# Spreading the reciprocal of the denominator by DMA, and moving den and M side by side, in a gated attention and MLP kernel

## The chip, the cores and the metric

The kernel runs on one core of one Trainium2 chip. The metric is the device time of one execution in microseconds (us); a time quoted for a kernel is the median of its runs. "Fast" is the undisturbed state of the chip; only fast runs are compared.

The engines: PE is TensorE's matrix products, PEld its weight loads, DVE is VectorE, ACT is ScalarE, POOL is GpSimd, and SP is the engine whose queue issues nearly all DMAs here.

## The reference, cut to what matters

```python
def _A_ref(x, wqkv, wo):                      # S = 2048, D = 640, 32 heads of 20
    ...
    pq, pk = phi(q), phi(k)
    kv  = jnp.einsum("bhsd,bhse->bhde", pk, v)
    z   = jnp.einsum("bhsd->bhd", pk)
    num = jnp.einsum("bhqd,bhde->bhqe", pq, kv)
    den = jnp.einsum("bhqd,bhd->bhq", pq, z)[..., None] + 1e-6
    o = num / den
    return (...o as [B, S, D]...) @ wo
def _B_ref(x, w1, w2, w3, w4): ...            # layernorm, W1, shift, W2, layernorm, W3, W4
g = sigmoid((x * gate_w).sum(-1))
out = g * _A_ref(...) + (1 - g) * _B_ref(...)
```

The division by `den` is one number for each head and token. The kernel computes the reciprocal as 32 rows (heads) times 2048 tokens, and needs it on all 128 partitions to scale `pq`: every head's row is wanted on four partitions. That spreading is what the change is about.

## The kernel before

Tokens are handled in four tiles of 512 (t = 0 to 3). PSUM is the memory that TensorE writes its results to. Below, den is the denominator, M is the product of each head's kv with `wo`, and W1 to W4 are the products of the MLP. The parts that the argument touches:

```python
ps = ctx.enter_context(tc.tile_pool(name="ps", bufs=4, space=PSUM))
def pair():                                    # a PSUM pair; four of them rotate
    return ps.tile([P, 2, 512], F32, name="pp")

def w1_unit(t, fcs):                           # 5 products of 512 columns for each fc, then gelu
    pt = pair()
    for i, fc in enumerate(fcs):
        for dc in range(DC):
            ...
            nc.tensor.matmul(pt[:, i, :], lhsT=w, rhs=lnxT[t][:, dc, :], ...)
    ...
def den_mm():                                  # 20 products, 32 columns of the array each
    pt = pair()
    for j in range(DC):
        for t in range(NT):
            nc.tensor.matmul(pt[32 * t:32 * (t + 1), 0, :], lhsT=zbd[:, j, :],
                             rhs=pqT[:, j, t * TS:(t + 1) * TS], ...)
    return pt
def den_evac(pt):
    nc.scalar.activation(pt[:, 1, :], pt[:, 0, :], ACT.Copy, bias=1e-6)
    nc.vector.reciprocal(r_bf[:], pt[:, 1, :])
def r_unit():                                  # 4 products, 32 rows of the array each
    pts = [pair(), pair()]
    for t in range(NT):
        nc.tensor.matmul(pts[t // 2][:, t % 2, :], lhsT=emat[32 * t:32 * (t + 1), :],
                         rhs=r_bf[32 * t:32 * (t + 1), :], start=True, stop=True)
    for k in range(2):
        nc.scalar.copy(rb[:, 2 * k:2 * k + 2, :], pts[k][:])
def m_unit(j):                                 # 16 products, 32 columns of the array each
    pt = pair()
    for hf in range(2):
        for p in range(2):
            for q in range(4):
                nc.tensor.matmul(pt[32 * q:32 * (q + 1), hf, 0:HD], lhsT=kvT[:, 2 * q + p, j, :], ...)
    nc.scalar.copy(m_sb[:, j, :]..., pt[:, :, 0:HD])
# cut: the order of the stretch in question
for fcs in w1_split:                           # W1 of tile 0: ((0, 1), (2, 3), (4,))
    w1_unit(0, fcs)
kv_unit()
den_evac(den_mm())
for cc in range(CPT):
    ln1_apply(3 * CPT + cc)                    # layernorm of tile 3, each ends in a DMA transpose
for fcs in w1_split:
    w1_unit(1, fcs)
...
for j in range(DC):
    m_unit(j)
r_unit()
# then W2 of tile 0, W1 of tiles 2 and 3 (scale_t multiplies pqT by rb on DVE), W3, ...
```

Three forms of TensorE's array are in play: the full array (W1, kv, W2), four tiles of 32 columns (den, M), and four tiles of 32 rows (the spreading products).

## Time and profile before

Time 265.61 us (three runs, 265.43 to 266.17). The page of the profile, its share of busy time, granted clock (in tenths, 40 slices) and the summary of the chain that ended last:

```profile
...
PE 260.3 (99%) x1744; PEld 161.8 (61%) x1744; DVE 139.5 (53%) x271; ACT 85.1 (32%) x126; POOL 21.9 (8%) x67
...
PEclk9999999999999999999999999999999999999999
...
PE 97%; ACT 1%; DVE 0%; issue 0%
...
```

TensorE is busy for 99% of the span at full clock, and 97% of the chain of waits is TensorE's. The list of waits of PE has one line (who waited for whom: us in total, times, longest):

```profile
...
PE pp L206 <- PEq L589: 0.8, 1, 0.8
```

The stretch that the change touches, from the timeline of PE (start in us, us until its last product ends, engine, line, operation, output<-inputs, shape, count). Products overlap, so lengths of stages are differences of starts:

```profile
...
71.28 4.48 PE L345 MATMUL pp<-lnxT,w_sb 128*128 128x512 bf16 x20
...
76.67 1.60 PE L364 MATMUL pp<-wk_sb,m_sb 128*128 128x120 bf16 x30
78.19 1.26 PE L251 MATMUL pp<-pqT,zbd 128*32 128x512 bf16 x20
79.39 4.49 PE L345 MATMUL pp<-lnxT,w_sb 128*128 128x512 bf16 x20
...
84.89 2.90 PE L383 MATMUL pp<-wo_sb,kvT 128*32 128x320 bf16 x80
87.72 0.40 PE L263 MATMUL pp<-r_bf,emat 32*128 32x512 bf16 x4
88.20 5.59 PE L417 MATMUL pp<-w_sb,hsT 128*128 128x320 bf16 x40
...
```

| Stage (before) | us between starts | products |
|---|---|---|
| W1 of tile 0 | 5.39 | 25 of 512 columns, 0.2156 each |
| kv | 1.52 | 30 |
| den | 1.20 | 20, four at a time |
| W1 of tile 1 | 5.50 | 25 |
| M | 2.83 | 80, four at a time |
| spreading products | 0.48 | 4, at once |
| whole stretch, W1 of tile 0 to W2 | 16.92 | |

The same place in the chain of waits (start, us, what):

```profile
...
84.96 0.69 PE pp L383 x16
85.65 0.02 issue
85.67 2.49 ACT m_sb L385 x4
88.16 0.04 issue
88.20 5.59 PE pp L417 x40
...
```

Here ACT stands in the chain: from 85.67 to 88.16 it goes over four of ACT's copies of M, into W2's start at 88.20.

DVE's timeline shows the reciprocal, and W2's first sum:

```profile
...
80.17 3.36 DVE L258 RECIPROCAL r_bf<-pp 128x512 bf16<-128x512 f32 x1
...
89.76 0.82 DVE L420 TENSOR_TENSOR x<-pp,x_sb 128x640 f32<-128x640 f32 x1 [2.94 <-PE pp L417]
...
```

SP's timeline shows the transposes of the first layernorm for tiles 2 and 3 (line 303), and those of the second layernorm of tile 0 (line 436):

```profile
...
74.63 16.46 SPq L303 DMA_TRANSPOSE lnxT<-ln  x8
94.58 6.89 SPq L436 DMA_TRANSPOSE lnxT<-ln  x4
...
```

### The profile page before, as it was taken

To read this page: it belongs to the slowest core of one execution; us is meant where nothing else is said; L and a number is where in the kernel's file an instruction comes from. 1 tells how busy PE (TensorE), PEld (TensorE's weight loads), DVE (VectorE), ACT (ScalarE), POOL (GpSimd) and SP (SyncE) were. 2 spreads that over 40 slices of the span, in tenths; PEclk is the share of its full clock that TensorE was granted. 3 is DMA by queue.
4 is the path that set the end of the run, shared out by engine and by line. 5 is a ranking of instruction groups with operands and counts; after the bars stand their busy time and mean duration, and the time that the engine had idled before them with its cause. 6 is when DMAs were issued, how large, how long until landed. Compare 5 with 4: busy or idle time off the path is not lost.

```text
span 264.0 us, 4272 instructions
## 1 busy us (share of the span) xinstructions
PE 260.3 (99%) x1744; PEld 161.8 (61%) x1744; DVE 139.5 (53%) x271; ACT 85.1 (32%) x126; POOL 21.9 (8%) x67
## 2 busy tenths in 40 slices
PE   8999999999999999999999999999999999999995
PEld 4777555788754654556667555667565576555743
DVE  1688778899948597964503455413356223112132
ACT  1555554321165725612502221412131332142100
POOL 7100120012210040001000001000001000000000
PEclk9999999999999999999999999999999999999999
DMA  7999987016673726700132000051100051100011
GB/s 200 179 208 370 375 252 298 0 29 123 124 101 75 79 51 161 239 0 2 25 75 77 25 0 2 0 99 52 50 0 2 0 101 52 50 0 2 0 50 50
DMA packets 46285, 23.62 MB, mean 89 GB/s; under 512 B 35770, under 2 KB 45626, under 8 KB 46266
## 3 DMA queue, kind: packets, MB, share of 16 engines
q1 hardware_dynamic: 45824, 22.86, 34.1%
q10 hardware_dynamic: 442, 0.49, 0.5%
q8 instruction: 13, 0.21, 0.4%
q14 instruction: 6, 0.05, 0.1%
HBM read 12.21 MB, written 2.62 MB: 56 GB/s over the span
## 4 chain that ended last, share of the span: by engine, by line
PE 97%; ACT 1%; DVE 0%; issue 0%
PE pp L484 21%; PE pp L464 21%; PE pp L194 8%; PE pp L311 8%; PE pp L417 8%; PE pp L448 8%; PE pp L345 8%; PE pp L236 8%; PE pp L206 2%; PE pp L472 1%; PE pp L493 1%; ACT m_sb L385 1%; PE pp L364 1%; PE pp L251 0%; DVE oc L512 0%; PE pp L383 0%
## 5 line engine op out<-in xcount | busy, mean ns | idle before, releaser
L464 PE MATMUL pp<-lnxT,w_sb 128*128 128x512 bf16 x260 | 60.4, 379 | 0.0
L484 PE MATMUL pp<-w_sb,h 128*128 128x256 bf16 (+3 forms) x416 | 58.0, 299 | 0.1
L466 ACT ACTIVATE h<-pp 128x1024 bf16<-128x1024 f32 (+1 forms) x28 | 26.9, 962 | 82.2 <-PE pp L464 82.2
L484 PEld LDWEIGHTS <-h 128*128 128x128 bf16 x416 | 39.3, 98 | 18.0 <-issue 1.3
L464 PEld LDWEIGHTS <-w_sb 128*128 128x128 bf16 x260 | 25.5, 98 | 26.8
L500 DVE SCALAR_TENSOR_TENSOR oc<-pp,omg,x 128x640 bf16<-128x640 f32 x14 | 12.0, 881 | 41.4 <-ACT h2x L475 21.3
L451 DVE SCALAR_TENSOR_TENSOR x<-pp,gate,x 128x640 f32<-128x640 f32 x16 | 13.9, 868 | 29.4 <-PE pp L448 29.4
L420 DVE TENSOR_TENSOR x<-pp,x_sb 128x640 f32<-128x640 f32 x16 | 13.1, 820 | 22.6 <-PE pp L417 22.6
L186 ACT ACTIVATE e<-pp 128x640 bf16<-128x640 f32 (+1 forms) x26 | 21.5, 827 | 9.6 <-PE pp L236 9.6
L448 PE MATMUL pp<-m_sb,pqT 128*128 128x320 bf16 x160 | 24.3, 299 | 0.0
L417 PE MATMUL pp<-w_sb,hsT 128*128 128x320 bf16 x160 | 23.9, 299 | 0.1
L194 PE MATMUL pp<-wk_sb,xT 128*128 128x320 bf16 (+1 forms) x160 | 22.9, 302 | 0.0
L311 PE MATMUL pp<-x_sb,pk 128*128 128x320 bf16 (+1 forms) x160 | 22.3, 300 | 0.0
L236 PE MATMUL pp<-xT,hsT 128*128 128x512 bf16 x100 | 21.7, 379 | 0.0
L311 PEld LDWEIGHTS <-pk 128*128 128x128 bf16 x160 | 18.8, 117 | 3.5
L417 PEld LDWEIGHTS <-hsT 128*128 128x128 bf16 x160 | 15.6, 98 | 8.2 <-issue 0.2
L448 PEld LDWEIGHTS <-pqT 128*128 128x128 bf16 x160 | 15.7, 98 | 7.7
L194 PEld LDWEIGHTS <-xT 128*128 128x128 bf16 x160 | 15.8, 99 | 6.1
L345 PE MATMUL pp<-lnxT,w_sb 128*128 128x512 bf16 x80 | 17.9, 379 | 0.0
L236 PEld LDWEIGHTS <-hsT 128*128 128x128 bf16 x100 | 11.8, 118 | 9.7
L281 POOL TENSOR_SCALAR rstd<-mv 128x4 f32<-128x4 f32 (+1 forms) x11 | 3.4, 314 | 156.5 <-DVE mv L287 156.5
L188 DVE SCALAR_TENSOR_TENSOR pk<-pp,e 128x640 bf16<-128x640 f32 x16 | 13.2, 825 | 1.7
(77 smaller groups left out, 194.9 us busy)
## 6 DMA issues: line engine op xcount, KB each, us to landing
out_dram<-oc SPq DMA_DIRECT2D x14, 160.0 KB, 1.8
w_sb<-in_B_w_dram SPq DMA_DIRECT2D x1, 2080.0 KB, 10.0
w_sb<-in_B_w_dram SPq DMA_DIRECT2D x1, 1296.0 KB, 8.4
x_sb<-in_A_x_dram SPq DMA_DIRECT2D x2, 640.0 KB, 10.4
x_sb<-in_A_x_dram SPq DMA_DIRECT2D x1, 1120.0 KB, 7.9
wo_sb<-in_A_wo_dram SPq DMA_DIRECT2D x6, 160.0 KB, 6.0
w_sb<-in_B_w_dram SPq DMA_DIRECT2D x1, 864.0 KB, 5.7
hsT<-in_A_wqkv_dram SPq DMA_DIRECT2D x1, 800.0 KB, 5.3
```

Of the source, the lines that this page charges most:

```text
L186: nc.scalar.activation(ev, src, ACT.Exp)
L188: nc.vector.scalar_tensor_tensor(dst, src, 0.0, ev, op0=ALU.max, op1=ALU.add)
L194: nc.tensor.matmul(pt[:, hf, 0:n], lhsT=xT[:, dc, c * P:(c + 1) * P], rhs=wk_sb[:, dc, hf * HD:hf * HD + n], start=(dc == 0), stop=(dc == ...
L236: nc.tensor.matmul(pt[:, t % 2, :], lhsT=wq_sb[:, dc, :].rearrange("p (m j) -> p j m", j=DC)[:, j], rhs=xT[:, dc, t * TS:(t + 1) * TS], st ...
L311: nc.tensor.matmul(pt[:, hf, 0:HD + hf], lhsT=w, rhs=x_sb[:, c, hf * HD:(hf + 1) * HD + hf], start=(c == 0), stop=(c == NCH - 1))
L345: nc.tensor.matmul(pt[:, i, :], lhsT=w, rhs=lnxT[t][:, dc, :], start=(dc == 0), stop=(dc == DC - 1))
L417: nc.tensor.matmul(pt[:, hf, 0:HD], lhsT=hsT[:, fc, 2 + c * P:2 + (c + 1) * P], rhs=w2_sb[:, fc, hf * HD:(hf + 1) * HD], start=(fc == 0), ...
L448: nc.tensor.matmul(pt[:, hf, 0:HD], lhsT=pqT[:, j, c * P:(c + 1) * P], rhs=m_sb[:, j, hf * HD:(hf + 1) * HD], start=(j == 0), stop=(j == D ...
L451: nc.vector.scalar_tensor_tensor(x1, pt[:, :, 0:HD], gate[:, c:c + 1], x1, op0=ALU.mult, op1=ALU.add)
L464: nc.tensor.matmul(pt[:, k, :], lhsT=w3_sb[:, dc, fc * P:(fc + 1) * P], rhs=lnT[:, dc, :], start=(dc == 0), stop=(dc == DC - 1))
L466: nc.scalar.activation(h2[:, 2 * i * TS:(2 * i + n) * TS], pt[:].rearrange("p h e -> p (h e)")[:, 0:n * TS], ACT.Gelu_apprx_tanh)
L484: nc.tensor.matmul(dst, lhsT=st[t]["h2"][:, fc * TS + cc * P:fc * TS + (cc + 1) * P], rhs=w4_sb[:, fc, a:b], start=start and fc == 0, stop ...
```

## The change

The intent is to take the four spreading products off the bottleneck engine: DVE copies the reciprocal's four bands into one tile of 32 partitions, and four DMAs write it to partitions i, i+4, i+8 and so on. Den and M are put side by side behind the first W1 unit of tile 1, so that the array keeps its form. Epsilon is added by DVE instead of ACT. Loads are merged, to make room for the four DMAs on SP.

```diff
 def den_evac(pt):
-    nc.scalar.activation(pt[:, 1, :], pt[:, 0, :], ACT.Copy, bias=1e-6)
+    d = e_p.tile([P, 1024], BF16, name="e")[:].bitcast(F32)
+    nc.vector.tensor_scalar_add(d, pt[:, 0, :], 1e-6)
-    nc.vector.reciprocal(r_bf[:], pt[:, 1, :])
-
-def r_unit():
-    ... (four products, two ACT copies)
+    nc.vector.reciprocal(r_bf[:], d)
+    for t in range(NT):
+        nc.vector.tensor_copy(r4[:, t, :], r_bf[H * t:H * (t + 1), :])
+    for i in range(4):
+        nc.sync.dma_start(rb[bass.ds(i, H, 4), :, :], r4[:])
 ...
 kv_unit()
+w1_unit(1, w1_split[0])
 den_evac(den_mm())
+for j in range(DC):
+    m_unit(j)
 for cc in range(CPT):
     ln1_apply(3 * CPT + cc)
-for fcs in w1_split:
+for fcs in w1_split[1:]:
     w1_unit(1, fcs)
 ...
-for j in range(DC):
-    m_unit(j)
-r_unit()
 ...  (cut: x, wv, w1 and w3 loaded in one DMA each where there were two;
       the masks emat gone; kvT's memset and the copies to w1x split otherwise)
```

More of the change, by code (lines that the diff above doesn't have):

```diff
@@ L85 @@
     r_bf = const.tile([P, TS], BF16)
+    r4 = const.tile([H, NT, TS], BF16)
     ident = const.tile([P, P], BF16)
@@ L90 @@
     zbd = const.tile([P, DC, H], BF16)
-    emat = const.tile([P, P], BF16)
     bmask = const.tile([P, GH * 4], F32)
@@ L136 @@
     load_x(1, 8)
-    load_x(8, 12)
-    load_x(12, 16)
-    for a, b in ((0, 2), (2, DC)):
-        sp.dma_start(wv_sb[:, a:b, :], wqkv_v[:, a:b, 2 * D:3 * D])
-    for a, b in ((0, 2), (2, DC)):
-        sp.dma_start(w1_sb[:, a:b, :], B_w1[a * P:b * P, :].rearrange("(c p) f -> p c f", p=P))
+    load_x(8, 16)
+    sp.dma_start(wv_sb[:], wqkv_v[:, :, 2 * D:3 * D])
+    sp.dma_start(w1_sb[:], B_w1.rearrange("(c p) f -> p c f", p=P))
     for g in range(NG):
@@ L147 @@
         sp.dma_start(w2_sb[32 * g:32 * (g + 1), 4, :], B_w2[CG * g + P:CG * (g + 1), :])
-    for a, b in ((0, 2), (2, DC)):
-        sp.dma_start(w3_sb[:, a:b, :], B_w3[a * P:b * P, :].rearrange("(c p) f -> p c f", p=P))
+    sp.dma_start(w3_sb[:], B_w3.rearrange("(c p) f -> p c f", p=P))
     nc.gpsimd.memset(mhalf[:], -0.5)
@@ L161 @@
                             base=3, pattern=[[4, H]], channel_multiplier=-1)
-    nc.gpsimd.memset(emat[:], 1.0)
-    for t in range(4):
-        sl = emat[32 * t:32 * (t + 1), :]
-        nc.gpsimd.affine_select(out=sl, in_=sl, compare_op=ALU.is_ge, fill=0.0,
-                                base=0, pattern=[[1, P]], channel_multiplier=-4)
-        nc.gpsimd.affine_select(out=sl, in_=sl, compare_op=ALU.is_ge, fill=0.0,
-                                base=3, pattern=[[-1, P]], channel_multiplier=4)
     for m, n, off in ((bmask, GH, 0), (bmask5, 2, 88)):
@@ L174 @@
                                 base=off + Dh - 1, pattern=[[Dh, n], [0, 4]], channel_multiplier=-1)
-    nc.gpsimd.memset(kvT[:], 0.0)
-    for a, b in ((0, 1), (1, 2), (2, 3), (3, DC)):
+    for b in range(0, len(pairs_qg), 2):
+        nc.gpsimd.memset(kvT[:, b:b + 2], 0.0)
+    for dc in range(DC):
         for g in range(4):
-            nc.gpsimd.tensor_copy(w1x[:, a:b, 32 * g:32 * (g + 1)], w1_sb[:, a:b, CG * g + P:CG * (g + 1)])
+            nc.gpsimd.tensor_copy(w1x[:, dc, 32 * g:32 * (g + 1)], w1_sb[:, dc, CG * g + P:CG * (g + 1)])
     def phi(dst, src, n):
@@ L255, in den_evac @@
     def den_evac(pt):
-        nc.scalar.activation(pt[:, 1, :], pt[:, 0, :], ACT.Copy, bias=1e-6)
+        d = e_p.tile([P, 1024], BF16, name="e")[:].bitcast(F32)
+        nc.vector.tensor_scalar_add(d, pt[:, 0, :], 1e-6)
         with nc.allow_low_precision(reason="rounded after a float32 division, as a copy would"):
-            nc.vector.reciprocal(r_bf[:], pt[:, 1, :])
-    def r_unit():
-        pts = [pair(), pair()]
+            nc.vector.reciprocal(r_bf[:], d)
         for t in range(NT):
-            nc.tensor.matmul(pts[t // 2][:, t % 2, :], lhsT=emat[32 * t:32 * (t + 1), :],
-                             rhs=r_bf[32 * t:32 * (t + 1), :], start=True, stop=True)
-        for k in range(2):
-            nc.scalar.copy(rb[:, 2 * k:2 * k + 2, :], pts[k][:])
+            nc.vector.tensor_copy(r4[:, t, :], r_bf[H * t:H * (t + 1), :])
+        for i in range(4):
+            nc.sync.dma_start(rb[bass.ds(i, H, 4), :, :], r4[:])
     def scale_t(t):
```

## The prediction

> **What bounds the kernel now.** TensorE. The page shows PE busy 260.3 of 264.0 us (99%) at a granted clock of 1.00; the chain that ended last is 97% PE; the list of waits shows one PE wait in the whole program, 0.8 us at the start. So only PE work, PE joints or a new PE wait change the time.
>
> **The stretch concerned**, read from the timeline of PE starts: W1 of tile 0 5.39 us, kv 1.52, den 1.20, W1 of tile 1 5.50, M 2.83, spread of the reciprocal (4 products) 0.48, W2 of tile 0 5.43.
>
> The four products each take 0.384 us but overlap: PE is busy 0.40 us with all four. The Trainium skill ("TensorE: Matmul & The Clock Gate", Part 3) says products on different 32-row groups run concurrently; this trace agrees. So they are worth 0.48 us, not 1.5.
>
> Joints: a W1 product is issued every 0.216 us, so 25 take 5.39; tile 1's W1 takes 5.50 after den. Den's five rounds of 4 should take 1.08, took 1.20. M's 20 rounds at 0.1357 should take 2.71, took 2.83. So entering or leaving the 32-column form costs about 0.1 us, and PEld sits idle 0.4 us at such places. Den beside M means one excursion, not two.
>
> **Removed:** the 4 products (0.48 us of PE, critical); three ACT copies (1.07, 1.07, 0.58) and masks on POOL: none critical.
>
> **Added:** DVE add of epsilon (estimate 0.65 us, from 0.82 for 640 float32 columns), four 32x512 copies (1.19 us, as the four hx copies take), four DMAs of 128 KB issued by SP (about 0.5 us each, landing within about 2 us). The reciprocal stays 3.36 us. The merged loads and split POOL copies run well before their readers: no effect.
>
> **New order in time:** the first W1 unit (2.16) covers the kvT masking (78.85 to 80.13), so M can start at once after den, near 81.6. DVE: add to 82.4, reciprocal to 85.8, copies to 87.0, four layernorms to 88.4, hx copies to 89.8, then W2's first sum at 89.8, as before (89.76). PE reaches W2 near 87.6 instead of 88.20. Hence:
> - Den's PSUM pair is freed near 82.4, needed near 83.3.
> - W2's fourth unit needs the hx copies near 92; they end near 89.8.
> - rb lands near 91; the scaling reads it after 101.
> - Tile 3's transposes are issued about 5 us later, near 88.5 to 94. Their reader, W1 of tile 3, starts near 98.4.
> - Tightest: the last transpose of tile 0's second layernorm was issued at 100.3 and lands 2.6 us later, 102.9; W3 started at 104.42, now near 103.9. Slack about 1 us, less if DVE slips.
>
> So I expect no new PE wait, and the saving to be the 0.48 us plus one joint, 0.5 to 0.7.
>
> **Predicted: 265.0 us, 264.3 to 265.7 (8 in 10). Chances: faster by over 2% 0.01, within 2% 0.97, slower by over 2% 0.02.**
>
> **What would show each step.** PE start of W2 near 87.6; PE busy lower by about 0.5 us; W3's first start about 0.5 to 0.6 us earlier; den plus M about 3.9 us together against 4.03 apart; the DVE scaling at about the same time as before (101.35).
>
> **What would make it wrong.** A PE wait for tile 3's or W3's first transposes (SP held by the rb DMAs, or rb DMAs colliding with transposes); W2 waiting for DVE; M waiting for kvT or den's pair. Each would cost about 0.5 to 3 us, under 2%. Run-to-run spread is 0.7 us.

## The result, and the profile after

The time after is 265.28 us (four runs, 265.21 to 265.60); before, with one more run, 265.73 us. Ratios in this document are the mean time of one kernel's fast runs over that of the other's fast runs of the same rounds, so not quite the ratio of the medians quoted. Here it is 0.9984, with a 95% interval of 0.9967 to 1.0001. The change was run again later (below): 265.26 against 265.91 us, ratio 0.9985 (0.9961 to 1.0010). So the change is within 2%, as predicted; the two ratios agree on about 0.4 us, each with an interval that just reaches 1.

The page after, busy time and the summary of the chain:

```profile
...
PE 258.4 (98%) x1722; PEld 161.0 (61%) x1740; DVE 141.4 (54%) x276; ACT 82.7 (31%) x123; POOL 20.2 (8%) x65
...
PE 92%; SPq 3%; DMA 3%; issue 1%; DVE 0%
...
```

PE's busy time fell by 1.9 us, but this number can't be used: 1722 products are on the record, where the change took away 4 of 1744. The others are records that the trace lacks. Starts of stages don't suffer from that. (The chain's 3% for SP and for DMA are from the first loads at the program's start, not from the stretch.)

PE's timeline after:

```profile
...
71.41 4.48 PE L332 MATMUL pp<-lnxT,w_sb 128*128 128x512 bf16 x19
...
76.81 1.60 PE L351 MATMUL pp<-wk_sb,m_sb 128*128 128x120 bf16 x30
78.25 2.32 PE L332 MATMUL pp<-lnxT,w_sb 128*128 128x512 bf16 x9
80.50 1.26 PE L241 MATMUL pp<-pqT,zbd 128*32 128x512 bf16 x20
81.59 2.89 PE L370 MATMUL pp<-wo_sb,kvT 128*32 128x320 bf16 x80
84.41 2.33 PE L332 MATMUL pp<-lnxT,w_sb 128*128 128x512 bf16 x9
...
87.66 5.60 PE L403 MATMUL pp<-w_sb,hsT 128*128 128x320 bf16 x40
...
103.88 2.32 PE L450 MATMUL pp<-lnxT,w_sb 128*128 128x512 bf16 x9
...
```

From W1 of tile 0 to W2 it is now 87.66 - 71.41 = 16.25 us, 0.67 us less than 16.92. Den takes 1.09 and M 2.82, together 3.91, where it was 1.20 and 2.83. W1 of tile 0 itself began 0.13 us later than in the profile of before, so W3 starts only 0.54 us earlier (103.88 against 104.42), and so does the end.

PE's list of waits has three lines more than before:

```profile
...
PE pp L184 <- DMA wk_sb<-in_A_wqkv_dram: 0.2, 1, 0.2
PE pp L470 <- issue: 0.2, 1, 0.2
PE pp L184 <- DMA xT<-in_A_x_dram: 0.2, 1, 0.2
```

The two waits for DMA are for the program's first loads (the first at 5.83 us), long before the stretch. The line with `issue` stands in all nine profiles that lack products and in none of the five that have them all, so it is most likely a gap in the record.

In the chain of waits ACT has gone from this place; between M and W2 there are products only:

```profile
...
81.76 2.72 PE pp L370 x80
...
87.82 5.43 PE pp L403 x40
...
```

DVE has the new addition, the reciprocal, and the copies; W2's first sum comes at the time it came before:

```profile
...
81.81 0.69 DVE L247 TENSOR_SCALAR e<-pp 128x512 f32<-128x512 f32 x1 [1.56 <-PE pp L241]
82.54 3.35 DVE L249 RECIPROCAL r_bf<-e 128x512 bf16<-128x512 f32 x1
85.93 1.17 DVE L251 COPY r<-r_bf 32x512 bf16<-32x512 bf16 x4
...
89.78 0.82 DVE L406 TENSOR_TENSOR x<-pp,x_sb 128x640 f32<-128x640 f32 x1
...
```

The reciprocal takes the same from SBUF as from PSUM (3.35 against 3.36 us). On SP, the four new DMAs (line 253), tile 3's transposes (line 290) and those of the second layernorm (line 422):

```profile
...
87.13 2.50 SPq L253 DMA_DIRECT2D rb<-r  x4
89.73 5.22 SPq L290 DMA_TRANSPOSE lnxT<-ln  x4
95.49 5.99 SPq L422 DMA_TRANSPOSE lnxT<-ln  x4
...
```

Each of the four DMAs holds SP for about 0.59 us and lands 2.6 to 3.4 us after its issue. Tile 3's transposes start at 89.73; the second layernorm's first transpose is issued at 95.49, after 94.58 before, because it now queues behind them. Its reader, W3, started without a wait.

### The profile page after: what moved, and what is told of

It is laid out like the page before. It is cut to its first block, busy times and chain, and to the rows that moved or that the text cites. A ratio compares the mean times of both kernels' runs of the same rounds, so it can differ in the third digit from the quotient of the medians.

```text
span 263.5 us, 4244 instructions
## 1 busy us (share of the span) xinstructions
PE 258.4 (98%) x1722; PEld 161.0 (61%) x1740; DVE 141.4 (54%) x276; ACT 82.7 (31%) x123; POOL 20.2 (8%) x65
## 4 chain that ended last, share of the span: by engine, by line
PE 92%; SPq 3%; DMA 3%; issue 1%; DVE 0%
PE pp L470 21%; PE pp L450 21%; PE pp L298 8%; PE pp L434 8%; PE pp L403 8%; PE pp L332 8%; PE pp L226 8%; PE pp L184 4%; DMA xT<-in_A_x_dram 3%; SPq L121 3%; PE pp L370 1%; PE pp L458 1%; PE pp L479 1%; PE pp L351 1%; PE pp L241 0%
## 5 line engine op out<-in xcount | busy, mean ns | idle before, releaser
L177 DVE TENSOR_SCALAR e<-e 128x640 bf16<-128x640 bf16 (+1 forms) x26 | 9.5, 367 | 8.9 <-ACT e L176 7.5
```

## The experiments

The first question is what the 0.67 us consist of. The theory: columns of the products, plus a fixed price each time the array changes its form. Rivals: all of it is the products, or it comes from the relief of ACT and DVE. The main measure is the stretch from the first W1 product of tile 0 to the first product of W2, because whole times turned out to carry noise from both ends of the program.

### Run 1: the DMA spread alone

```diff
 (kernel before)
     nc.vector.reciprocal(r_bf[:], pt[:, 1, :])
+    (the four copies and the four DMAs)
-r_unit()
```

> Kernel before, with only the four spreading products and their two ACT copies replaced by the four DVE copies and four DMAs; den and M stay apart. Theory (the gain is PE work plus joints of the array's form): the four products and the joint between row form and full form go, the exit joint of M stays: W2 starts 0.45 to 0.5 us earlier relative to the start of W1 of tile 0 than in before (16.4 against 16.92 us), time 0.4 to 0.5 us less. Rival A (all of the gain is the products): the whole 0.67 us. Rival B (the gain comes from ACT or DVE relief): anything else.

The stretch was 88.17 - 71.72 = 16.45 us, 0.47 us shorter than before. So the products with what hangs on them are worth 0.47, not the whole 0.67. The time, however, was 265.83 us against 265.80, ratio 1.0007 (0.9988 to 1.0026): the expected 0.4 to 0.5 us was not seen, and the interval leaves room for 0.3 us at most. In this profile the program's end took 0.7 us longer; runs 10 and 12 return to that.

### Run 2: the order alone

```diff
 (kernel after)
-    (the four copies and the four DMAs)
+def r_unit(): ... (as before)
 for fcs in w1_split[1:]:
     w1_unit(1, fcs)
+r_unit()
```

> Kernel after, but the reciprocal is spread by the four products again, right before W2; den and M stay side by side behind the first W1 unit of tile 1. Theory: two joints less than before, stretch from W1 of tile 0 to W2 16.7 us or a little less (0.2 us less than 16.92), and the four products again 0.4 to 0.5 us. Rival A: 16.92, no gain from order.

The stretch was 88.05 - 71.39 = 16.66 us, 0.26 less than before; time 265.98, ratio 1.0012 (0.9995 to 1.0029). The products cost less here than in before. PE's timeline of this run, the products and W2:

```profile
...
87.73 0.39 PE L261 MATMUL pp<-r_bf,emat 32*128 32x512 bf16 x4
88.05 5.61 PE L415 MATMUL pp<-w_sb,hsT 128*128 128x320 bf16 x40
...
```

That is 0.32 us from their start to W2's, where 0.4 to 0.5 was expected and before had 0.48 for the very same four products.

### Runs 3 and 5: the products four times, and twice

```diff
 (kernel before)
-    for t in range(NT):
+    for t in list(range(NT)) * 4:      # and * 2
         nc.tensor.matmul(pts[t // 2][:, t % 2, :], lhsT=emat[...], rhs=r_bf[...], ...)
```

> Kernel before, with the four spreading products issued four times over (same result). Theory: four concurrent products cost the columns of one, 0.216 us, and the rest of their 0.48 us is the joint, paid once: each of the three extra rounds adds 0.22 us, 0.65 us in all (0.48 becomes 1.13). Rival: the 0.48 us is all cost of the products, then 1.4 us more; if they were not concurrent, 2.6 us more.

> Kernel before, with the four spreading products issued twice. The run with four rounds added 0.50 us to the stretch, not 0.65, and its chain of waits has no ACT piece, where that of before goes over four ACT copies of M (2.49 us) into W2. Theory (in before W2 waits about 0.15 us for ACT to free the PSUM pair of M's fourth unit, and a second round of products hides in that wait): M to W2 0.216 times 2 plus 0.12, 0.55 us against 0.48, only 0.07 more. Rival (each round simply costs 0.167): 0.65 us.

The timelines of PE, first with four rounds:

```profile
...
88.17 1.04 PE L263 MATMUL pp<-r_bf,emat 32*128 32x512 bf16 x16
89.15 5.61 PE L417 MATMUL pp<-w_sb,hsT 128*128 128x320 bf16 x40
...
```

and with two:

```profile
...
87.61 0.61 PE L263 MATMUL pp<-r_bf,emat 32*128 32x512 bf16 x8
88.15 5.61 PE L417 MATMUL pp<-w_sb,hsT 128*128 128x320 bf16 x40
...
```

Four rounds take 0.98 us, two 0.54, one took 0.48. So four rounds added 0.50 us and not the expected 0.65. From two to four it is 0.22 us for each round, one product's 512 columns; from one to two only 0.06. So with one round some 0.15 us of PE's time was no work. The chain of waits names it: in before it goes over ACT's copies of M into W2, with two and four rounds there is no ACT in that place. Four PSUM pairs rotate; W2's first unit takes the pair of M's fourth unit, and before waited for ACT to empty it. A second round of products hides in that wait. The weight loads show the same wait directly. The timeline of weight loads (PEld) in before has W2's first one at 88.05:

```profile
...
88.05 0.93 PEld L417 LDWEIGHTS <-hsT 128*128 128x128 bf16 x7 [0.23 <-issue]
```

W2's first product started at 88.20, 0.15 us after it; in runs 1, 2, 3 and 5, which change form there too, the two starts lie within 0.01 us of each other. It was not less work on ACT that removed the wait: in run 1 ACT's copies of M began 14.39 us after W1 of tile 0, just as in before, and W2 started at 88.17, before the fourth of them had ended (near 88.6).

The rival, 0.167 us for each round, is refuted by the run with two rounds (0.54 measured, 0.65 expected). Time with four rounds 266.64, ratio 1.0033 (1.0017 to 1.0050), which is the 0.5 us of the stretch and some noise.

### Run 4: M put apart again

```diff
 (kernel after)
-for j in range(DC):
-    m_unit(j)
 ...
-for fcs in w1_split[1:]:
-    w1_unit(1, fcs)
+for fc in (2, 3, 4):
+    w1_unit(1, (fc,))
+    m_unit(fc - 2)
+for j in (3, 4):
+    m_unit(j)
```

> Kernel after, but den, the first three M units and the last two are put apart by five or ten W1 products each (three W1 units of one PSUM half), so the array enters and leaves the 32-column form four times instead of once. Theory (0.2 us for one entry and exit): three more excursions, the stretch from W1 of tile 0 to W2 grows from 16.25 to about 16.85 us, time 0.6 us more than after. Rival (joints cost nothing, the saving came from elsewhere): 16.25 and the time of after.

The stretch was 88.32 - 71.42 = 16.90 us, 0.65 more than after, for three more entries and exits. PE's timeline around two of them:

```profile
...
82.89 0.73 PE L370 MATMUL pp<-wo_sb,kvT 128*32 128x320 bf16 x16
83.55 1.25 PE L332 MATMUL pp<-lnxT,w_sb 128*128 128x512 bf16 x5
84.73 0.73 PE L370 MATMUL pp<-wo_sb,kvT 128*32 128x320 bf16 x16
...
```

An M unit of 16 products should take 4 x 0.1357 = 0.54 (0.1357 us is what a W2 product of 320 columns takes, four M products go at once); it takes 0.66. Five W1 products should take 1.08; they take 1.18. The time was 265.68, ratio 1.0002 (0.9976 to 1.0027): against the 265.28 of after, from another job, this is 0.4 us more, in line, but not resolved by so few runs.

With this the stretch can be written as a sum. Its work is 50 W1 products at 0.2156, kv 1.43 (the chain's number), five rounds of den at 0.2156, 20 rounds of M at 0.1357: 16.00 us, plus 0.22 for each round of spreading products. The rest, divided by the changes of form:

| Kernel | stretch, us | work, us | rest, us | changes of form | rest for each |
|---|---|---|---|---|---|
| after | 16.25 | 16.00 | 0.25 | 2 | 0.12 |
| order alone | 16.66 | 16.22 | 0.44 | 4 | 0.11 |
| DMA spread alone | 16.45 | 16.00 | 0.45 | 4 | 0.11 |
| products twice | 16.99 | 16.43 | 0.56 | 5 | 0.11 |
| products four times | 17.43 | 16.86 | 0.57 | 5 | 0.11 |
| M apart | 16.90 | 16.00 | 0.90 | 8 | 0.11 |
| before | 16.92 | 16.22 | 0.70 | 5 | 0.14 |

Six kernels agree on 0.11 to 0.12 us for each change of form. Before is the only one out of line, by 0.70 - 5 x 0.112 = 0.14 us: the wait for ACT. So the 0.67 us are 0.22 of columns, three changes of form (0.33), and the lost wait (0.14); these add up to 0.69. A change of stage that keeps the form costs almost nothing: in after, den to M takes 1.09 us for 1.08 of work, and the last W1 unit to W2 1.08 for 1.08. Before was profiled once, so its 0.48 rests on one profile; its stages up to the products (16.44 us) agree with runs 3 and 5 (16.45 each).

### Run 6: epsilon back in PSUM

```diff
 (kernel after)
-    d = e_p.tile(...); nc.vector.tensor_scalar_add(d, pt[:, 0, :], 1e-6)
-    nc.vector.reciprocal(r_bf[:], d)
+    nc.scalar.activation(pt[:, 1, :], pt[:, 0, :], ACT.Copy, bias=1e-6)
+    nc.vector.reciprocal(r_bf[:], pt[:, 1, :])
```

> Kernel after, but epsilon is added by ACT within PSUM and the reciprocal reads PSUM, as in before. Theory (DVE's add only frees a PSUM pair early; the built program lets M rotate over the three other pairs, and W2's first unit waits for the reciprocal, done near 85.8): no PE wait, W1 of tile 0 to W2 16.25 us as after, 0 to 0.2 us longer if an ACT copy is late. Rival (M's fourth unit must wait for the reciprocal): 2.4 us longer.

The stretch was 87.69 - 71.44 = 16.25 us and the time 265.30 us, ratio 0.9981 (0.9962 to 0.9999), the same as after. Moving epsilon to DVE is worth nothing here, in either direction. The wait that one would fear, M's fourth unit for den's pair, does not come.

### Run 7: the old loads

```diff
 (kernel after)
-    (merged loads of x, wv, w1, w3; split memset and w1x copies)
+    (those of before)
```

> Kernel after, with the loads, the memset and the w1x copies of before. Theory (these parts run long before their readers): stage times and W1's start as in after apart from the start of the program, where four runs put W1 of tile 0 at 71.28 to 71.72 whatever the kernel; time within 0.3 us of after. Rival (merged loads shift the start): W1 of tile 0 starts at 71.28 as in before, the two early waits for DMA of after (0.2 us each) are gone.

The stretch was 16.25 us again. W1 of tile 0 started at 71.69, so the start was not the one of before, and the early waits of after are not tied to merged loads either (one of them was seen in the run with the products twice, which has the old loads). The time was 265.69, ratio 0.9992 (0.9970 to 1.0014), 0.4 us more than after and so just outside the expected 0.3, and again the program's end was 0.7 us longer.

### Runs 8 and 11: the four DMAs three times, and twice

This measures how much slack SP's queue had.

```diff
 (kernel after)
-    for i in range(4):
+    for i in list(range(4)) * 3:       # and * 2
         nc.sync.dma_start(rb[bass.ds(i, H, 4), :, :], r4[:])
```

> Kernel after, with the four DMAs of the reciprocal issued three times (same result), to measure the slack of the SP queue behind them. Each DMA costs SP 0.59 us to issue, and each round waits for the landing of the round before, so tile 3's transposes should be issued 5 to 5.5 us later, near 95 to 100, the last landing near 101.7; W1 of tile 3, which would start at 98.5, then waits about 3 us, and W3 starts about 3 us later. If the queue had more slack than I think: no wait and the time of after.

> Kernel after with the four DMAs issued twice. From the run with three rounds (last transpose of tile 3 landed near 102.7, each extra round about 2.8 to 3.3 us): tile 3's transposes issued near 92.6 to 97.8, the last landing near 99.2, so W1 of tile 3 waits 0.3 to 0.8 us, W3 up to 0.8 us later than in after. A wait this short should leave the granted clock at 1.0, where the wait of 3.8 us took it to 0.994 and made the next twenty products 1.4 us longer.

PE's timeline with three rounds, W1 of tile 3:

```profile
...
102.78 5.92 PE L332 MATMUL pp<-lnxT,w_sb 128*128 128x512 bf16 x20 [3.82 <-DMA lnxT<-ln]
...
```

with two rounds:

```profile
...
100.25 4.48 PE L332 MATMUL pp<-lnxT,w_sb 128*128 128x512 bf16 x20 [1.47 <-DMA lnxT<-ln]
...
```

With two rounds the wait was 1.47 us, more than expected, because SP needed 6.3 us for eight issues with their waits, not 5. The first transpose of tile 3 was issued 3.83 us later than in after (93.56 against 89.73), and W1 of tile 0 had itself started 0.14 us later, so the slack was 3.83 - 0.14 - 1.47 = 2.2 us. With three rounds the same sum gives 6.20 - 0.31 - 3.82 = 2.1 us. So the change has spent most of the slack of tile 3's transposes, and about 2 us are left.

With three rounds W3 started at 109.61, 5.7 us later than in after (about 3 was expected), though the wait was 3.8. The view of windows, for the wait and for the stretch after it (window; busy us and instructions of PE, PEld, DVE, ACT and POOL; granted clock; share of DMA busy; GB/s):

```profile
...
98.96:102.78 3.82, 0.00 (x1) 0.03 (x1) 3.55 (x7) 0.64 (x2) 0.93 (x2) 0.94 0.62 123
102.78:108.53 5.75, 5.75 (x20) 2.30 (x21) 4.86 (x12) 1.09 (x2) 1.16 (x3) 0.74 0.53 104
...
```

The twenty products after the wait took 5.75 us instead of 4.31, at a mean granted clock of 0.74 (0.50 up to 105.5 us, 1.00 from 106.0 on). With two rounds, after a wait of 1.47 us, they took 4.31 at 1.00. The Trainium skill ("TensorE: Matmul & The Clock Gate", Part 1, "What's actually happening") says that the clock falls to half after an idle window of about 3.4 us; both runs, one profile each, are in line with it. The times of these single runs were 270.92 and 267.63 us.

### Runs 9, 10 and 12: the time again, and the program's ends

> Kernel after once more, unchanged, for the time and the spread at both ends. Theory: W1 of tile 0 to W2 16.25 us again; W1 of tile 0 starts anywhere from 71.2 to 71.7 (TensorE's first products run slow for a time that differs from run to run), W3 to the end of the span 159.6 to 160.3; time 0.3 to 0.7 us less than before, ratio 0.997 to 0.999.

> The kernel with the DMA spread alone once more, which saved 0.47 us in its stretch and nothing in the time of its first four runs. Theory (the time of that job lost the gain to the start and the end, which differ from run to run): stretch 16.45 us again, time 0.2 to 0.5 us less than before, between before and after. Rival (the DMA spread costs something outside of the stretch when done alone): time equal to before again, and a stage of the profile outside of start and end is longer.

> The DMA spread alone, but with the merged loads of after, so that SP has as many DMAs as in before (96 in the two runs with the spread alone and the old loads, 92 here and in before). In eleven profiles the time from DVE's last operation to the end of the span was 2.3 us in all seven kernels with 92 SP DMAs, 3.0 us in the three runs with 96 and the old loads. Theory (the DMA spread is worth its 0.47 us, and the program's end, which follows SP's stream and not the work, took it back): stretch 16.45 us, end 2.3 us, time 0.3 to 0.6 us less than before, ratio about 0.998. Rival (the spread alone itself makes the end longer): end 3.0 us again, time equal to before.

Run 9 is the kernel after, unchanged. Run 10 is the kernel of run 1, unchanged. Run 12 has this edit:

```diff
 (kernel of run 1, DMA spread alone)
-    (x, wv, w1 and w3 loaded in two DMAs each: 96 DMAs on SP)
+    (the merged loads of the changed kernel: 92 DMAs on SP, as in before)
```

Run 9 repeated the change: stretch 16.24, time 265.26 (six runs, 265.04 to 267.14) against 265.91.

Runs 10 and 12 repeated the stretch of the DMA spread alone, 87.49 - 71.04 = 16.45 and 87.40 - 70.95 = 16.45, and neither is measurably faster than before: 265.95 against 265.91, ratio 0.9997 (0.9985 to 1.0009), and 265.75 against 266.05, ratio 0.9996 (0.9983 to 1.0009). So neither shows the expected 0.2 to 0.6 us; the intervals leave room for at most 0.40 and 0.45 us. The two ends of the program explain why such a gain is hard to see:

- The start. TensorE's first products run slow, for a time that differs: two products of 320 columns took 0.54 us at 4.82 in before and 0.28 at 6.08, but 0.27 already at 4.72 in run 12. (The granted clock on record reads 1.00 there all the same; the slow phase is read from the products' starts.) In fourteen profiles W1 of tile 0 started anywhere from 70.95 to 71.72 us, and kernels with the same code up to there (before, and the products twice and four times) have 71.28, 71.16 and 71.72. The skill describes such a start (same page and section: the activity window runs freely, so the point of change varies by 500 ns either way). Waits for the first loads can add to it: the profile of after has two of 0.2 us.
- The end. From DVE's last operation to the end of the span it takes 2.3 us in before, after, and five other kernels, but 3.0 or 3.1 in runs 1, 7 and 10, 2.7 in run 12, 2.6 in runs 2 and 11.

SP's list of waits shows the end. Its last two waits (us in total, times, longest), before, then run 10:

```profile
...
SPq L600 <- DMA out_dram<-oc: 0.8, 1, 0.8
...
SPq L600 <- PEq L600: 0.6, 2, 0.4
...
```

```profile
...
SPq L588 <- DMA out_dram<-oc: 1.1, 1, 1.1
SPq L588 <- PEq L588: 1.0, 2, 0.5
...
```

The wait for the last output's DMA grew from 0.8 to 1.1 us, and that for PE's sequencer from 0.6 to 1.0. Both are after all work is done. I had guessed that this follows the number of DMAs on SP, because all seven profiles with 92 had the short end, and the three with 96 and the old loads the long one. Run 12 has 92 and an end of 2.7 us, with the first wait short (0.8) and the second long (1.0). So the guess is at best half right; what sets the end in a given build stays open. It does not touch the change: before and after both have the short end of 2.3 us.

One run of before took 705.72 us; it was slow and is not used.

No version better than the changed kernel came out of this. What is left in the stretch over the bare work is 0.25 us, two changes of form; run 6 equals the changed kernel.

## Why the prediction was right

The predicted time was 265.0 us, 264.3 to 265.7; measured 265.28. The class, within 2%, was right, but says little: any change of less than 5 us would have met it, and the interval of the time reaches 1. The evidence is the stretch. There the mechanism was right for most points:

- **TensorE bounds.** Right. In the profiled runs the span fell by 0.5 us, the stretch's 0.67 less the 0.13 of its later start, and nothing of the relief of ACT and POOL shows elsewhere. Run 6 shows it for the ACT operation with epsilon.
- **Size in the stretch, 0.5 to 0.7 us.** Right, 0.67. The split was less good. "So they are worth 0.48 us" took the whole gap from the products' start to W2's as a cost of the products. It was 0.22 of columns, 0.14 of waiting for ACT to free a PSUM pair, and a change of form. The wait stood in the chain of waits before ("ACT m_sb L385 x4", 2.49 us), and I had not used it: the list of waits has no line for it, since the products' modelled ends cover all but 0.08 us of the gap. "The list of waits shows one PE wait in the whole program" was true of the list and not of the kernel. That the sum came out right was partly luck: the wait and the change of form, not known to be part of the 0.48, went away together with the products (run 1 saved 0.47).
- **Joints of about 0.1 us.** Right: 0.11 to 0.12 for each change of form. Three fewer give 0.33 us, where the prediction counted one excursion at about 0.1 to 0.2 beside the products; the change of form that went with the products was hidden in their 0.48.
- **No new PE wait.** Right; runs 8 and 11 show that about 2 us of slack are left for tile 3's transposes. The prediction called W3's transposes the tightest place with about 1 us; with the DMAs doubled, W1 of tile 3 was the first to wait, for 1.47 us, and W3 waited only 0.2 us after it.
- **Times of the stages.** W2 at 87.66 (predicted 87.6), W3 at 103.88 (103.9), den plus M 3.91 (3.9), W2's first sum on DVE at 89.78 (89.8). Tile 3's transposes came at 89.73 instead of 88.5, behind SP's four DMAs, which were first issued at 87.13 and took 2.5 us, where I had counted 2; even with 2 us, from copies done at 87.0, the prediction's own numbers give 89.0. The DVE scaling came at 101.37 (before 101.35), as predicted.
- **PE busy lower by about 0.5 us.** Not usable: 1.9 us lower, with products missing from the record.
- **The spread between runs.** "Run-to-run spread is 0.7 us" was taken as noise of no origin. Two parts of it were found: the slow first products at the start, and the program's end, which differs between builds.

The time came out 0.3 us above the predicted one. In the profiled run 0.13 us of that is the later start of the stretch; the rest is within the spread, and not explained.

## What to carry to other kernels

On a kernel bound by TensorE, small products on tiles of the array cost their columns once for four, plus about 0.11 us for every change of the array's form around them; put those of one form side by side, and count changes as carefully as products. A gap between two stages on a busy engine is not all work: look in the chain of waits for another engine before you price it, and double the suspected cost, as a wait shows by swallowing the first addition. For gains below the noise of whole times, compare a stretch within the profile that begins and ends at fixed products.

## What the Trainium skill lacked or had wrong

- "TensorEngine Tiling (Array Packing)", Key Properties, says that changing the tiling mode drains TensorE, without a price. The runs give 0.11 to 0.12 us for each change (2, 4, 5 and 8 changes in six kernels), between the full array, tiles of 32 columns and tiles of 32 rows.
- "TensorE: Matmul & The Clock Gate", Part 3, table of measured speedup, has 3.07 for four row tiles of 512 columns. Here a further round of four cost 0.22 us, as one full product does (0.2156): a speedup of 4 in a stream, if four in turn would cost four full products (an estimate; none ran in turn here). The single round in run 2 took 0.32 us with its change of form, by the same estimate 2.7 times faster. The table does not say which of the two it measures.
- "DMA: Bandwidth & Descriptors" has a fit of 2.0 us plus bytes over 436 GB/s (fitted on another DMA path), which by estimate gives 2.3 us for 128 KB. The four DMAs from SBUF to SBUF, issued one right after another, landed 2.6 to 3.4 us after issue, and each held the issuing queue for 0.59 us.
- "Runtime: NRT & Kernel Launch" gives the first barrier after the kernel one figure, about 1.5 us. Here the time from DVE's last operation to the end of the span, which holds the last output's DMA and the engines' last waits for each other (the trace does not show whether these are that barrier), was 2.3 to 3.1 us: different between builds of nearly the same kernel, and the same when a build was profiled again (3.0 twice, 2.3 twice). The difference is as large as the whole gain studied here, and no page warns of it.
